# Twenty small filling matmuls instead of eight large ones at TensorE's start, and another order behind them

## The chip, the core and the metric

The kernel runs on one core of a Trainium2 chip. The metric is the time of one execution on the device, in microseconds. Lower is better. A core has five engines that run side by side, each taking its own instructions in order: TensorE (PE; its weight loads are listed as PEld), VectorE (DVE), ScalarE (ACT), GpSimd (POOL) and SyncE (SP), which here issues all transfers between HBM and the on-chip memory.

## What is computed

```python
def _attn_ref(q, k, v, f_logit):          # each [4, 8, 768, 48]
    f = 1.0 / (1.0 + np.exp(-f_logit))
    for t in range(S):
        state = f[:, :, t, :, None] * state + np.einsum('bhd,bhe->bhde', k[:, :, t], v[:, :, t])
        y[:, :, t] = np.einsum('bhd,bhde->bhe', q[:, :, t], state)
    return y

def _moe_ref(x, w_in, w_out):             # x [3072, 384], w_in [384, 2048], w_out [2048, 384]
    h = x @ w_in
    g = np.maximum(0.01 * h, h)
    return (g @ w_out).astype(np.float32)
```

A gated linear recurrence runs over 768 time steps for 4 batches and 8 heads. Its output, with the heads side by side, is the input x of a two-layer network with a leaky ReLU. Inputs and outputs are float32.

## The kernel before, in words

**Units.** The recurrence is done in chunks of 128 steps: within a chunk as a masked product of scores, between chunks by a state per head. The work is cut into 12 units j of 256 rows of x. Units 0 to 3 ("paired") hold the first two chunks of one batch each; units 4 to 11 hold one chunk of two batches.

**Steps of a unit.** Each has a short name, and the number of the unit comes next in it. `Lf`, `Lk`, `Lq`, `Lv` load f, k, q, v (SP; lines 158 and 162). `ge` and `gl` make the logarithm of the gate (ACT, 236 and 248). `cs` sums it up along time on TensorE (257 to 268), `dec` turns the sums into decays (ACT, 276 to 285). `k` and `q` scale k and q by them (301, DVE or POOL); `v` casts v (307 to 316, POOL or ACT). The scaled k and q are transposed, for units 0 to 3 on TensorE (`tk`, `tq`, line 335) with a copy from PSUM behind it (`ck`, `cq`, 348 ACT or 350 DVE), for the others by a DMA (`xk`, `xq`, 355). `sc` are the scores (371, 378), `mk` their masking (DVE, 388, 392), `pt` the chunk's addition to the state (482, 487), `sf` and `sb` the new state and its cast (497 to 508). `mx` mixes masked scores and v, and the old state (409); in a paired unit the part of the second chunk that reads the first chunk's state is a step of its own, `ms`. `xt` copies the result to xT (469 ACT, 471 DVE).

**The network.** `up_j_g` multiplies two of 16 column blocks of w_in (six matmuls of 256 columns, line 516), `pr_j_g` is the leaky ReLU (ACT, 521), `dn_j_a_n` multiplies a quarter of w_out into the output of half a (four matmuls of 384 columns, 528), `ob` copies the output (ACT 572, DVE 574), `st` stores it (578). The last half is split in two (`dh`, `oh`, `sh`; 550 to 564).

**Weights.** `WI_0` to `WI_4` load pieces of w_in of 256, 256, 512, 512 and 512 columns, `WO_0` to `WO_3` quarters of w_out. The first two pieces have buffers of their own, the others pass through a ring of three: WI_2, WI_3, WI_4, then WO_0, WO_1, WO_2, WO_3 in the slots that come free. `cw_0_c` casts 256 columns of w_in and `cw_1_c` half a quarter of w_out; the last number names the engine (0 DVE, 1 ACT, 2 POOL; lines 199 and 201). From block 2 on, an `up` needs both halves of its piece: up_j_2 and up_j_3 wait for cw_0_2 and cw_0_3.

**The filling.** `id_n@b` makes TensorE multiply a constant tile by itself, n times 128 columns into bank b, at most 512 columns in one matmul (line 207). Nothing reads the result. id_30 is thus 8 matmuls, id_1 is one.

**Order.** Nothing is scheduled by a planner at run time or by the framework: a string named `order` lists every step, and each engine gets its instructions in that order. Numbers after @ are the PSUM banks that a step writes; there are eight banks, and a step waits until the last reader of its bank is done. Every product is two TensorE instructions, a weight load and a matmul. An instruction's index below is its place in TensorE's list, counted so.

```python
    for word in order.split():
        word, _, on = word.partition("@")
        name, *numbers = word.split("_")
        parts[name](*[int(n) for n in numbers], *[int(n) for n in on.split(".") if n])
```

Of the kernel before, what the change touches and what calls it, by code (L numbers as in the profile page):

```python
# [15 lines left out]
def kernel(  # L16
# [592 lines left out]
    dec_3_0 Lf_4_1 dn_0_1_1 cw_1_5_1 cw_1_4_2 dn_1_0_1 up_0_7@1 dn_1_1_1 pr_0_7 pt_2_2@7.3 Lq_3_2 mx_2_2@6.1
    cw_1_6_1 cw_1_7_2 sf_2_0 dn_1_0_2 Lv_3_2 xt_2_0_1 k_3_1_1 dn_0_0_1 Lf_5_0 dn_1_0_3 sb_2_0_0 dn_0_1_2 Lf_5_1  # L610
    k_3_0_1 ob_1_0_1 sf_2_1 ge_4_2 tk_3_1@7 dn_0_0_2 ck_3_1_0 sb_2_1_1 Lv_4_0 ms_2 gl_4_2 dn_0_0_3 q_3_1_0
    xt_2_1_1 tk_3_0@6 q_3_0_0 ob_0_0_1 dn_0_1_3 ck_3_0_0 Lv_4_1 cs_4_0@0 ob_0_1_0 tq_3_1@3 v_3_0_0 dec_4_0
    cs_4_1@7 cq_3_1_0 tq_3_0@1 Lk_4_0 up_2_0@5 cq_3_0_0 dec_4_1 v_3_1_0 up_2_1@6 Lk_4_1 pr_2_0 dn_1_1_2 pr_2_1
    Lq_4_0 sc_3_0@4.3 ge_5_2 sc_3_1@0.1 mk_3_0_0 pt_3_2@7.5 Lk_5_0 gl_5_2 up_2_2@6 sf_3_0 dn_1_1_3 mk_3_1_1
    sb_3_0_0 Lq_4_1 pr_2_2 up_2_7@4 mk_3_1_0 ob_1_1_1 v_4_2_0 Lq_5_0 mk_3_0_1 cs_5_1@7 cs_5_0@1 pr_2_7
    dn_2_1_0@6 sf_3_1 dec_5_0 Lk_5_1 mx_3_2@0.2 k_4_2_0 sb_3_1_0 up_2_5@3 xt_3_0_0 ms_3 pr_2_5 up_2_3@4 st_0_0
    xt_3_1_0 pt_4_0@5 Lq_5_1 pt_4_1@1 pr_2_3 dn_2_0_0@0 sf_4_0 dec_5_1 q_4_2_0 dn_2_1_1 sb_4_0_0 xk_4 up_2_6@3
    sf_4_1 up_2_4@2 st_0_1 pr_2_6 sb_4_1_1 dn_2_0_1 pr_2_4 up_3_1@4 xq_4 dn_2_1_2 pr_3_1 k_5_2_0 q_5_2_1 Lf_6_0
    dn_2_0_2 Lf_6_1 dn_2_1_3 xk_5 dn_2_0_3 ob_2_1_1 up_3_0@5 ob_2_0_0 xq_5 up_3_2@7 pr_3_0 up_3_4@1 pr_3_2
    Lv_5_1 up_3_5@3 pr_3_4 ed_5 up_3_3@2 pr_3_5 sc_4_2@4.6.0.5 pr_3_3 Lv_5_0 dn_3_0_0@7 ge_6_2 mk_4_1_1  # L620
    dn_3_1_0@1 mk_4_0_1 Lf_7_0 gl_6_2 up_3_6@3 mk_4_1_0 Lf_7_1 mk_4_0_0 up_3_7@2 pr_3_6 st_1_0 dn_3_0_1 pr_3_7
    Lf_8_0 cs_6_0@5 v_5_2_0 sc_5_2@6.0.4.3 dec_6_0 Lf_8_1 cs_6_1@2 mk_5_1_0 dn_3_1_1 dec_6_1 Lk_6_1 mk_5_1_1
    dn_3_0_2 ge_7_2 mk_5_0_0 dn_3_1_2 mk_5_0_1 gl_7_2 mx_4_2@5.4 Lk_6_0 mx_5_2@3.2 Lv_6_0 xt_4_1_0 xt_4_0_0
# [30 lines left out]
    dn_10_1_1 up_11_7@2 up_10_7@6 pr_11_7 up_11_3@7 pr_10_7 up_11_0@1 pr_11_3 up_10_6@5 pr_11_0 up_11_5@3
    pr_10_6 up_11_2@2 pr_11_5 up_11_1@6 pr_11_2 up_10_4@7 pr_11_1 up_11_6@1 pr_10_4 dn_11_0_0@5 pr_11_6
    dn_10_0_2 dn_11_0_1 dn_10_1_2 dh_11_1_0@3 dn_10_1_3 oh_11_1_0_1 sh_11_1_0 dn_11_0_2 ob_10_1_0 dn_10_0_3
    st_10_1 dn_11_0_3 ob_10_0_1 dh_11_1_1 st_10_0 ob_11_0_1 st_11_0 oh_11_1_1_0 sh_11_1_1
# [35 lines left out]
```

## Time and profile before

| | |
|---|---|
| median of 3 runs | 178.19 us (177.94 to 178.99) |
| the profiled execution's own time | 178.71 us |
| its span, first to last instruction | 176.9 us |
| PE busy | 170.5 us (96%) |
| ACT busy | 122.5 us (69%) |
| DVE busy | 94.6 us (53%) |
| POOL busy | 52.5 us (30%) |
| filling matmuls (L207) | 37, 10.6 us |

Times in the profile count from the first instruction of the span. A row of the timeline has the start, the length, the engine, the line, the operation, the tiles (out<-in), the sizes and the number of instructions; what stands in brackets is the engine's idle time just before it and what ended it, where "issue" means that the engine waited for nothing that the profile shows. The chain of waits is followed back from the last instruction. Matmuls are pipelined, so their ends, and with them PE's busy time, are modelled; the start of the next matmul is the better mark.

### The profile page before, as it was taken

Reading aid. Unit: us, or ns where it says so; the run is one execution under the profiler, and the core shown is the slowest. Engines: PE = TensorE matmul, PEld = TensorE weight load, DVE = VectorE, ACT = ScalarE, POOL = GpSimd, SP = SyncE. Lnnn points to the kernel's source line nnn. Section 1 sums busy time; section 2 is a strip of 40 time slices with the busy share of each in tenths; the row PEclk is TensorE's granted clock in tenths of the full one; section 3 lists DMA queues with packets and bytes.
Section 4 is the critical chain, followed back from the end, with each engine's and each line's share of the span. In section 5 each row is a group of like instructions: output and inputs, shape, how many; then the busy total and the mean of one; then the engine's idle time right before and its main releaser. Section 6 shows DMA issues by size and latency. Waiting matters only on the chain.

```text
span 176.9 us, 5560 instructions
## 1 busy us (share of the span) xinstructions
PE 170.5 (96%) x2301; PEld 130.5 (74%) x2301; DVE 94.6 (53%) x201; ACT 122.5 (69%) x238; POOL 52.5 (30%) x102
## 2 busy tenths in 40 slices
...
GB/s 128 269 302 292 372 325 312 391 335 228 177 190 206 181 190 118 215 199 210 197 203 146 227 185 195 166 229 199 185 206 182 182 262 65 4 133 0 4 66 112
DMA packets 106856, 34.44 MB, mean 195 GB/s; under 512 B 101072, under 2 KB 105040, under 8 KB 106832
## 3 DMA queue, kind: packets, MB, share of 16 engines
...
q8 instruction: 18, 0.29, 0.7%
q14 instruction: 6, 0.05, 0.1%
...
## 4 chain that ended last, share of the span: by engine, by line
PE 89%; DMA 3%; ACT 3%; SPq 2%; issue 1%; DVE 0%; DVEq 0%
PE ps L516 36%; PE ps L528 35%; PE ps L409 6%; DMA f_raw<-in_f_logit_dram 3%; PE ps L378 3%; SPq L158 2%; PE ps L265 2%; PE ps L550 2%; PE ps L335 1%; PE ps L487 1%; PE ps L371 1%; ACT f_raw L236 1%; ACT lf L248 1%; PE ps L482 1%; PE ps L257 1%
## 5 line engine op out<-in xcount | busy, mean ns | idle before, releaser
L521 ACT ACTIVATE gT<-ps 128x512 bf16<-128x512 f32 x96 | 55.9, 602 | 24.4 <-PE ps L516 21.6
L516 PE MATMUL ps<-xT,w_in 128*128 128x256 bf16 x576 | 69.7, 273 | 0.0
L528 PE MATMUL ps<-w_out,gT 128*128 128x384 bf16 x368 | 68.4, 326 | 0.0
L516 PEld LDWEIGHTS <-w_in 128*128 128x128 bf16 x576 | 60.6, 110 | 5.3
L528 PEld LDWEIGHTS <-gT 128*128 128x128 bf16 x368 | 34.3, 98 | 18.9
L392 DVE TENSOR_TENSOR wm<-ps,ut 128x512 bf16<-128x512 f32 x32 | 20.0, 684 | 9.6 <-ACT gT L521 6.7
L307 POOL CAST vb<-v_raw 128x768 bf16<-128x768 f32 (+1 forms) x14 | 10.0, 713 | 43.5 <-DMA v_raw<-in_v_dram 43.4
L574 DVE COPY osb<-ps 128x384 f32<-128x384 f32 x12 | 6.7, 557 | 25.5 <-PE ps L528 24.8
L301 DVE TENSOR_TENSOR qh<-q_raw,at 128x384 bf16<-128x384 f32 (+1 forms) x14 | 10.3, 758 | 13.4 <-DMA q_raw<-in_q_dram 9.4
L301 POOL TENSOR_TENSOR kh<-k_raw,em 128x768 bf16<-128x768 f32 (+1 forms) x6 | 8.5, 1422 | 18.4 <-DMA k_raw<-in_k_dram 14.6
L236 ACT ACTIVATE f_raw<-f_raw 128x384 f32<-128x384 f32 (+1 forms) x16 | 10.8, 686 | 3.7 <-DMA f_raw<-in_f_logit_dram 3.7
L276 ACT ACTIVATE em<-ps 128x384 bf16<-128x384 f32 x24 | 11.8, 493 | 2.1 <-PE ps L265 0.9
L499 DVE TENSOR_TENSOR sf<-sf,ps 64x192 f32<-64x192 f32 x32 | 11.2, 350 | 3.4 <-PE ps L487 2.6
L508 POOL CAST sb<-sf 64x192 bf16<-64x192 f32 x26 | 10.3, 396 | 6.4 <-DVE sf L497 4.9
L277 ACT ACTIVATE at<-ps 128x384 bf16<-128x384 f32 x24 | 11.9, 498 | 0.0
L572 ACT COPY osb<-ps 128x384 f32<-128x384 f32 x11 | 5.3, 478 | 9.5 <-PE ps L528 8.7
L207 PE MATMUL ps<-warm 128*128 128x512 bf16 (+3 forms) x37 | 10.6, 409 | 1.1 <-DVE warm L83 1.1
L388 DVE TENSOR_TENSOR wm<-ps,pair_mask 128x512 bf16<-128x512 f32 x16 | 10.1, 685 | 2.8 <-PE ps L371 2.7
L471 DVE CAST xT<-ps 128x384 bf16<-128x384 f32 x12 | 6.5, 561 | 9.4 <-PE ps L409 9.3
L248 ACT ACTIVATE lf<-f_raw 128x384 bf16<-128x384 f32 (+1 forms) x16 | 10.8, 682 | 0.4
L505 POOL TENSOR_TENSOR sf<-sf,end 128x192 f32<-128x192 f32 x10 | 7.9, 794 | 7.1 <-PE ps L528 4.6
L469 ACT CAST xT<-ps 128x384 bf16<-128x384 f32 x12 | 6.3, 534 | 4.9 <-PE ps L409 4.9
...
## 6 DMA issues: line engine op xcount, KB each, us to landing
...
ring<-in_moe_w_out_dram SPq DMA_DIRECT2D x4, 768.0 KB, 7.3
...
ring<-in_moe_w_in_dram SPq DMA_DIRECT2D x3, 768.0 KB, 9.6
...
```

The lines of the kernel that those rows point to most:

```text
L207: nc.tensor.matmul(banks[bank][:, 0:128 * m], warm, warm[:, None, :].to_broadcast([128, m, 128]), start=True, stop=True)
L236: nc.scalar.activation(gates(j)[:, part], gates(j)[:, part], AF.Exp, scale=-1.0)
L248: nc.scalar.activation(dst, src, AF.Ln, bias=1.0)
L276: nc.scalar.activation(ems[j % 2][:, a], t[:, 0:H * D], AF.Exp, scale=1.0)
L277: nc.scalar.activation(ats[j % 2][:, a], t[:, 0:H * D], AF.Exp, scale=-1.0)
L301: eng.tensor_mul(heads(j, to[j % NR], a)[:, :, :, 0:D], raw_heads(j, x, a), decays(j, by, a))
L392: nc.vector.tensor_mul(w, src.rearrange("t (p n) -> t p n", p=P2), ut[:, None, :].to_broadcast([128, P2, 128]))
L409: nc.tensor.matmul(banks[st[j]["py", i]][32 * r:32 * r + 32, 128 * kk:128 * kk + 128], lhsT, rhs, start=(i, r) not in begun, stop=i in las ...
L499: nc.vector.tensor_add(sf[rows], sf[rows], new)
L516: nc.tensor.matmul(pm[:, i, :], w_in_of(ff, kk), xTs[j % 3][:, kk].rearrange("t a s -> t (a s)"), start=(kk == 0), stop=(kk == NK - 1))
L521: nc.scalar.activation(gTs[j % 3][:, 2 * g:2 * g + 2, :], pm, AF.Prelu, alpha=0.01)
L528: nc.tensor.matmul(po, gTs[j % 3][:, ff, 128 * a:128 * a + 128], w_out_b[quarter][:, ff % 4, :], start=(ff == 0), stop=(ff == NF - 1))
```

## The change

The first filling, one step of 30 x 128 columns in 8 matmuls, becomes 17 steps with the same columns in 20 matmuls: 16 of 128 columns, then 14 x 128 columns in four. TensorE has 12 products, 24 instructions, more before its first real one. The other fillings change too: after them all there are 45 filling matmuls instead of 37, with 13,696 columns instead of 17,024. The rest of the list has the same steps in another order, with other banks and here and there another engine: ACT gets two casts of half a v and one of a whole v more, and two xT copies and an output copy fewer; POOL gets one scaling of half a q more and one of a whole k fewer. Only the string changes. Its beginning, as far as the first two quarters of w_out, is below; the part behind it is a new order of the same steps, with no filling in either.

```diff
-    Lf_0_1 Lf_0_0 Lk_0_1 Lq_0_0 Lq_0_1 ge_0_1 Lk_0_0 gl_0_1 ge_0_0 id_30@6 cs_0_1@0 gl_0_0 dec_0_1 cs_0_0@1
-    Lv_0_2 k_0_1_0 Lf_1_2 dec_0_0 Lk_1_2 q_0_0_0 Lq_1_2 q_0_1_0 id_32@6 tq_0_0@2 k_0_0_0 cq_0_0_1 id_3@6
-    tq_0_1@3 tk_0_1@4 cq_0_1_1 tk_0_0@5 Lf_2_2 ck_0_1_0 ck_0_0_0 v_0_1_1 v_0_0_0 id_3@0 sc_0_1@6.7 sc_0_0@0.1
-    mk_0_1_1 WI_0 id_2@4 pt_0_2@2.3 mk_0_0_0 ge_1_0 sf_0_0 gl_1_0 WI_1 ge_1_1 id_13@5 cs_1_0@4 mk_0_0_1 sb_0_0_0
-    gl_1_1 mk_0_1_0 dec_1_0 id_5@7 cs_1_1@5 k_1_0_0 mx_0_2@7.0 dec_1_1 k_1_1_0 ms_0 xt_0_0_1 tk_1_0@2 Lv_1_2
-    tk_1_1@1 ck_1_0_1 q_1_0_0 xt_0_1_1 q_1_1_0 WI_2 id_7@4 tq_1_0@6 ge_2_1 cq_1_0_0 id_3@5 tq_1_1@4 WI_4 ge_2_0
-    ck_1_1_0 sf_0_1 cw_0_0_2 gl_2_0 cq_1_1_1 WI_3 sb_0_1_1 gl_2_1 id_19@2 sc_1_1@5.7 cw_0_1_1 sc_1_0@2.0
-    mk_1_1_1 cs_2_1@6 Lq_2_2 cs_2_0@1 mk_1_1_0 v_1_1_1 v_1_0_0 up_0_0@3 mk_1_0_0 dec_2_1 pt_1_2@4.7 mk_1_0_1
-    up_0_1@5 pr_0_0 Lk_2_2 sf_1_0 dec_2_0 mx_1_2@2.6 sb_1_0_1 pr_0_1 cw_0_2_0 cw_0_3_1 sf_1_1 id_16@3 ms_1
-    xt_1_0_1 sb_1_1_1 up_0_2@0 WO_0 xt_1_1_1 cw_0_7_0 up_0_3@3 pr_0_2 cw_0_6_0 up_1_1@4 pr_0_3 Lf_3_2 up_1_3@1
-    pr_1_1 cw_0_4_2 up_1_2@5 cw_0_5_1 up_1_0@7 pr_1_3 pr_1_2 up_0_6@2 WO_1 pr_1_0 up_1_6@6 q_2_0_0 pr_0_6
-    q_2_1_0 Lv_2_2 up_1_7@0 pr_1_6 k_2_1_0 up_1_5@3 pr_1_7 k_2_0_0 tq_2_0@4 pr_1_5 tq_2_1@1 cq_2_0_0 tk_2_1@5
-    WO_2 up_0_4@7 cq_2_1_0 cw_1_0_1 cw_1_1_2 ck_2_1_0 tk_2_0@2 up_1_4@6 pr_0_4 ck_2_0_0 WO_3 sc_2_1@0.3 ge_3_0
...
+    Lf_0_1 Lf_0_0 Lk_0_1 Lk_0_0 Lq_0_0 ge_0_1 Lq_0_1 gl_0_1 ge_0_0 id_1@6 id_1@6 id_1@6 id_1@6 id_1@6 id_1@6
+    id_1@6 id_1@6 id_1@6 id_1@6 id_1@6 id_1@6 id_1@6 id_1@6 id_1@6 id_1@6 id_14@6 cs_0_1@0 gl_0_0 dec_0_1
+    cs_0_0@1 Lv_0_2 k_0_1_0 Lf_1_2 dec_0_0 id_11@6 tk_0_1@2 k_0_0_0 Lk_1_2 ck_0_1_1 q_0_0_0 id_9@6 tk_0_0@3
+    Lq_1_2 ck_0_0_1 id_5@6 tq_0_0@4 q_0_1_0 cq_0_0_1 id_5@6 tq_0_1@5 Lf_2_2 sc_0_0@6.7 cq_0_1_0 v_0_0_1 v_0_1_0
+    sc_0_1@0.1 mk_0_1_1 WI_0 id_5@4 pt_0_2@2.3 mk_0_0_0 ge_1_0 mk_0_1_0 gl_1_0 Lv_1_2 ge_1_1 id_13@5 cs_1_0@4
+    sf_0_0 gl_1_1 mk_0_0_1 dec_1_0 sb_0_0_0 id_5@1 cs_1_1@5 k_1_0_0 mx_0_2@1.6 dec_1_1 k_1_1_1 xt_0_0_0 id_3@2
+    tk_1_0@0 WI_1 ms_0 q_1_1_1 xt_0_1_0 WI_2 ck_1_0_0 q_1_0_0 ge_2_0 WI_4 ge_2_1 id_21@7 tq_1_0@2 gl_2_0
+    tk_1_1@7 cw_0_0_2 cq_1_0_0 tq_1_1@4 gl_2_1 ck_1_1_0 sc_1_0@5.1 cq_1_1_1 WI_3 up_0_0@6 mk_1_0_0 v_1_1_1
+    v_1_0_0 sc_1_1@0.2 mk_1_0_1 Lk_2_2 pr_0_0 pt_1_2@7.4 cw_0_1_2 mk_1_1_1 cs_2_1@5 sf_1_0 cs_2_0@1 dec_2_1
+    mk_1_1_0 up_0_1@6 sb_1_0_0 Lq_2_2 mx_1_2@2.7 cw_0_3_1 cw_0_2_0 sf_1_1 ms_1 xt_1_0_1 up_0_2@0 pr_0_1 xt_1_1_0
+    sb_1_1_0 dec_2_0 up_0_3@5 sf_0_1 WO_0 up_1_2@2 pr_0_2 cw_0_6_2 cw_0_7_1 up_1_3@4 sb_0_1_0 pr_1_2 up_1_0@6
+    pr_0_3 up_1_7@7 pr_1_3 cw_0_5_0 up_1_1@3 pr_1_0 cw_0_4_1 up_0_6@1 pr_1_7 up_0_7@0 WO_1 pr_0_6 Lf_3_2
+    up_1_4@2 k_2_0_0 pr_1_1 k_2_1_0 Lv_2_2 up_1_6@5 pr_0_7 q_2_0_0 pr_1_4 tk_2_1@4 tk_2_0@6 q_2_1_0 ck_2_1_1
+    tq_2_0@7 up_0_5@1 ck_2_0_0 pr_1_6 cq_2_0_0 WO_2 tq_2_1@3 pr_0_5 up_0_4@0 cw_1_0_2 cq_2_1_0 cw_1_1_1
+    sc_2_0@2.4 sc_2_1@6.5 pr_0_4 mk_2_0_0 up_1_5@7 WO_3 mk_2_1_1 dn_0_1_0@1 cw_1_3_1 cw_1_2_2 mk_2_1_0
+    dn_1_1_0@3 pr_1_5 Lk_3_2 mk_2_0_1 dn_0_0_0@0 ge_3_1 ge_3_0 dn_0_1_1 gl_3_1 Lf_4_1 gl_3_0 dn_1_0_0@2 v_2_1_0
...
```

More of the change, by code (lines that the diff above doesn't have):

```diff
@@ L609 @@
[L609 to L623, printed above, removed]
@@ L654 @@
[L654 to L657, printed above, removed]
+    Lf_0_1 Lf_0_0 Lk_0_1 Lk_0_0 Lq_0_0 ge_0_1 Lq_0_1 gl_0_1 ge_0_0 id_1@6 id_1@6 id_1@6 id_1@6 id_1@6 id_1@6
@@ new lines @@
+    ge_5_2 ob_0_0_0 Lk_4_0 cs_4_1@5 pr_2_1 pt_3_2@4.3 dec_4_1 sc_3_1@1.7 Lk_4_1 sf_3_0 sc_3_0@0.6 dn_1_0_3
+    gl_5_2 mk_3_0_1 sb_3_0_0 Lq_5_0 cs_4_0@4 mk_3_1_0 ge_6_2 dn_2_1_0@5 mk_3_1_1 Lq_5_1 dec_4_0 cs_5_0@6
+    up_2_3@1 mk_3_0_0 gl_6_2 up_2_7@7 Lk_5_0 q_4_2_1 ob_1_0_0 mx_3_2@4.0 sf_3_1 pr_2_3 pr_2_7 cs_5_1@2 xt_3_0_0
+    ms_3 dec_5_0 sb_3_1_0 cs_6_1@1 Lk_5_1 xt_3_1_0 cs_6_0@3 dn_2_1_1 k_4_2_0 st_0_1 dn_2_0_0@7 dec_5_1 Lv_4_0
+    dn_2_1_2 q_5_2_0 up_2_6@4 Lv_4_1 dec_6_1 dn_2_0_1 pr_2_6 up_3_1@0 dec_6_0 up_3_0@6 xk_4 k_5_2_0 pr_3_1
@@ new lines @@
+    up_4_1@3 xt_5_1_0 Lk_6_0 sb_4_1_0 gl_7_2 sf_5_0 dn_2_0_3 Lk_6_1 pr_4_1 xt_5_0_0 up_4_4@2 sb_5_0_0 ge_8_2
+    ob_3_0_0 Lk_7_1 cs_7_1@5 sf_5_1 cs_7_0@6 pr_4_4 up_4_0@3 gl_8_2 ob_2_0_0 sb_5_1_0 up_5_1@4 pr_4_0 Lk_7_0
+    up_4_2@0 pr_5_1 q_6_2_0 cs_8_1@1 Lq_7_0 pr_4_2 dn_4_0_0@2 dec_7_0 up_5_2@7 Lq_7_1 k_6_2_1 up_4_3@3 xq_6
+    dn_4_1_0@4 pr_5_2 pr_4_3 up_5_6@0 dec_7_1 xk_6 cs_8_0@6 k_7_2_0 dn_4_0_1 dn_4_1_1 Lv_6_0 pr_5_6 Lv_6_1
+    up_5_7@7 dec_8_0 q_7_2_0 up_4_5@3 pr_5_7 st_2_0 up_5_5@5 dec_8_1 up_5_0@0 pr_4_5 xk_7 up_5_4@6 pr_5_5 pr_5_0
@@ new lines @@
+    up_4_6@7 pr_5_4 dn_4_0_2 pr_4_6 st_2_1 up_5_3@1 xq_7 sc_6_2@3.5.0.6 v_6_2_0 pr_5_3 dn_5_0_0@7 mk_6_1_1
+    Lv_7_1 dn_4_1_2 mk_6_0_0 Lv_7_0 up_4_7@1 Lf_9_1 mk_6_1_0 mk_6_0_1 dn_5_0_1 pr_4_7 ed_7 dn_5_1_0@6 pt_6_1@3
+    dn_4_1_3 Lf_9_0 sf_6_1 dn_5_1_1 ob_4_1_1 sb_6_1_1 st_3_1 dn_4_0_3 v_7_2_0 Lv_8_0 dn_5_1_2 ob_4_0_0 st_3_0
+    sc_7_2@0.5.1.3 Lk_8_0 mx_6_2@4.2 mk_7_1_1 Lv_8_1 mk_7_0_0 dn_5_1_3 xt_6_0_1 mk_7_0_1 Lk_8_1 xt_6_1_1
+    dn_5_0_2 Lq_8_0 ge_9_2 mk_7_1_0 pt_7_0@3 pt_7_1@0 pt_6_0@4 sf_7_0 ob_5_1_1 up_6_2@2 Lq_8_1 gl_9_2 sf_7_1
@@ new lines @@
+    sb_7_0_0 up_6_1@5 pr_6_2 sf_6_0 up_6_6@1 pr_6_1 sb_6_0_1 up_6_0@6 Lq_9_1 pr_6_6 v_8_2_0 cs_9_0@3 Lq_9_0
+    cs_9_1@0 pr_6_0 dn_5_0_3 dec_9_0 mx_7_2@2.4 k_8_2_1 Lk_9_0 ob_5_0_0 dn_6_1_0@5 xt_7_1_0 Lk_9_1 dec_9_1
+    xt_7_0_0 up_6_3@1 sb_7_1_0 q_8_2_0 xk_8 up_7_3@6 pr_6_3 up_6_5@7 pr_7_3 q_9_2_1 up_7_6@3 pr_6_5 up_7_0@4
+    xq_8 pr_7_6 pt_8_1@2 pt_8_0@0 pr_7_0 dn_6_0_0@1 sf_8_1 sf_8_0 dn_6_1_1 xq_9 k_9_2_1 sb_8_1_1 up_6_4@6
+    dn_6_0_1 pr_6_4 st_4_1 st_4_0 sb_8_0_0 up_7_4@7 xk_9 dn_6_0_2 pr_7_4 dn_6_1_2 Lf_10_0 up_7_1@3 Lf_10_1
@@ new lines @@
+    Lk_11_1 sf_9_1 gl_11_2 dn_7_1_3 sb_9_0_0 xt_9_0_0 Lk_11_0 xt_9_1_1 up_8_3@4 ob_7_1_1 k_10_2_0 up_8_7@0
+    sb_9_1_0 Lq_11_1 pr_8_3 cs_11_1@6 cs_11_0@5 pr_8_7 up_8_5@7 dec_11_1 up_9_3@2 Lq_11_0 pr_8_5 up_9_4@3
+    q_10_2_0 pr_9_3 xk_10 up_9_0@1 dec_11_0 up_9_7@4 pr_9_4 xq_10 k_11_2_0 pr_9_0 up_8_1@0 pr_9_7 up_9_1@6
+    pr_8_1 Lv_11_1 up_8_0@7 pr_9_1 Lv_11_0 q_11_2_0 up_8_2@2 pr_8_0 up_9_5@5 st_6_1 pr_8_2 dn_9_1_0@3 pr_9_5
+    xk_11 dn_8_1_0@1 dn_9_0_0@4 st_7_1 dn_8_1_1 up_8_6@0 up_9_2@6 xq_11 pr_8_6 v_11_2_0 up_8_4@7 pr_9_2 st_6_0
@@ new lines @@
+    up_9_6@2 pr_8_4 dn_9_1_1 pr_9_6 sc_10_2@5.0.6.7 dn_8_1_2 mk_10_0_1 dn_9_1_2 mk_10_0_0 dn_8_1_3 mk_10_1_1
+    mk_10_1_0 dn_9_1_3 ob_8_1_1 dn_9_0_1 st_8_1 ob_9_1_1 st_7_0 dn_8_0_0@2 st_9_1 dn_9_0_2 mx_10_2@0.5
+    sc_11_2@7.6.1.3 xt_10_1_1 xt_10_0_0 dn_8_0_1 mk_11_0_0 dn_9_0_3 mk_11_1_0 dn_8_0_2 mk_11_1_1 ob_9_0_1
+    mk_11_0_1 up_10_5@0 st_9_0 dn_8_0_3 pr_10_5 up_10_3@5 ob_8_0_1 mx_11_2@7.1 st_8_0 pr_10_3 up_10_1@3
+    xt_11_0_1 xt_11_1_0 up_10_7@4 pr_10_1 up_10_4@6 pr_10_7 up_11_6@0 pr_10_4 up_10_0@2 pr_11_6 up_11_1@5
```

51 lines of the change are left out of this document (19 added, 32 removed).

## The prediction

> **What bounds the kernel now.** I read the page first, then the busy time by stage, then the chain of waits at the border between the stages.
>
> ```profile
> span 176.9 us, 5560 instructions
> PE 170.5 (96%) x2301; PEld 130.5 (74%) x2301; DVE 94.6 (53%) x201; ACT 122.5 (69%) x238; POOL 52.5 (30%) x102
> q8 instruction: 18, 0.29, 0.7%
> ...
> 12.50:24.20 11.70, 9.97 (x265) 7.00 (x265) 10.22 (x25) 10.87 (x28) 1.69 (x4) 1.00 1.02 337
> 24.20:60.00 35.80, 35.80 (x527) 28.23 (x528) 22.27 (x49) 30.38 (x59) 16.41 (x31) 1.00 0.99 257
> 60.00:120.00 60.00, 60.00 (x749) 47.38 (x747) 34.43 (x60) 43.55 (x80) 21.57 (x33) 1.00 0.95 190
> 120.00:173.75 53.75, 53.72 (x652) 41.80 (x650) 17.66 (x30) 28.81 (x53) 8.65 (x13) 1.00 0.58 125
> ```
>
> The columns of the stage rows are length, then busy time of PE, PEld, DVE, ACT, POOL, granted clock, DMA share, GB/s. From 24.2 us to 173.75 us TensorE has no idle time: 149.52 of 149.55 us. Before that it waits (9.97 of 11.70 us busy in the stretch before), and a part of the busy time is the filling matmuls of L207. So the time is a sum of two: the moment T at which the dense stretch begins, and 149.6 us of work, then a tail of 3.2 us (output copy, store, end).
>
> In the border between the stages the chain of waits shows the place at which the change aims:
>
> ```profile
> 21.03 0.63 PE ps L409 x52
> 21.66 0.98 issue
> 22.64 0.30 PE ps L409 x10
> 22.95 0.97 PE ps L207 x4
> ...
> 24.20 6.67 PE ps L516 x60
> ```
>
> Inside the second mix (mx_1_2, L409) TensorE stands still for 0.98 us with "issue" as the reason: no semaphore holds it. Queue q8 brings 18 packets, 0.29 MB, that is 16 KB each; 4602 TensorE instructions over 18 packets are 256 a packet, so q8 brings TensorE's code in blocks of 256. Counting in the order, a weight load and a matmul for each product, the stall is at instruction 703: 594 come before mx_1_2, and 109 of it had been issued. Behind it comes a filling (id_16, 0.97 us) and only then ms_1 and up_0_2, the first instruction of the dense stretch, at 24.13 by the timeline.
>
> **The change, part by part.**
>
> *The sum after T.* All that TensorE does before up_0_2 is the same set of real steps in both orders, and so is all after it: 252 steps, no filling in either, and 41 changes between shapes of matmul in either order (counted). Such a change costs about 0.1 us:
>
> ```profile
> 97.29 0.65 PE ps L528 x4
> ...
> 98.49 0.89 PE ps L409 x56
> 99.38 0.76 PE ps L528 x4
> ```
>
> The same four matmuls of L528 take 0.65 us behind L516, whose tile has the same shape, and 0.76 behind a mix (L409). With equal counts the dense sum stays 149.6 us. Bounds: below, nothing, since 149.52 of it is busy; above, new waits (rivals).
>
> *The first filling.* 8 matmuls of 3,840 columns become 16 of 128 and 4 of 1,792 columns together: again 3,840 columns, 12 matmuls more.
>
> ```profile
> 1.06 3.38 PE L207 MATMUL ps<-warm 128*128 128x512 bf16 x8 [1.06 <-DVE warm L83]
> 1.46 0.15 PEld L207 LDWEIGHTS <-warm 128*128 128x128 bf16 x1 [0.28 <-issue]
> 3.99 0.52 ACT L248 ACTIVATE lf<-f_raw 128x384 bf16<-128x384 f32 x1
> 4.56 0.32 PE L257 MATMUL ps<-lf,bu 128*128 128x192 bf16 x1
> ```
>
> It ends at 4.44, the logarithm that the first cumulative sum needs at 4.51. If the extra weight loads hide, the new filling lasts 3.4 us too: cost 0. If they don't, 12 x 0.15 = 1.8 us come on top, the first sum starts 1.7 us late. I take 0: 8 x 512 columns' loads were hidden here, and eight 128-column transposes with eight loads took 0.63 us later (below), 80 ns a pair.
>
> [...]
>
> *The code block.* The 24 instructions more at the front shift all later numbers; with the other fillings changed, mx_1_2 now begins at 618 instead of 594. Instruction 703 is then the 43rd matmul of the same mix, not another step. The block edge before it, at 703 - 256 = 447, moves from the score of unit 1 (sc_1_1) to the transpose before it (tq_1_0). Before, TensorE reached that edge at 17.56 and went on at 22.64, 5.1 us later:
>
> ```profile
> 17.56 0.64 PE L371 MATMUL ps<-qT,kT 48*64 48x128 bf16 x32 [0.75 <-ACT qT L348]
> 22.35 0.69 DVE L201 CAST w_in<-ring 128x768 bf16<-128x768 f32 x1 [0.56 <-DMA ring<-in_moe_w_in_dram]
> 22.35 0.83 ACT L199 CAST w_in<-ring 128x768 bf16<-128x768 f32 x1
> 23.85 0.35 PE L409 MATMUL ps<-qT,sb 128*32 128x128 bf16 x12
> 24.13 0.30 PE L516 MATMUL ps<-xT,w_in 128*128 128x256 bf16 x1
> ```
>
> The new order reaches tq_1_0 at 16.5 (shown below), so the code is there between 21.7 (the same 5.1) and 22.64 (if the request goes out no earlier than before, or the DMA queue alone sets the time). Take the late end: 21 matmuls of the mix are left (0.3 us), then ms_1 (0.28 us, 23.85 to 24.13): 23.2.
>
> *The weights.* up_0_2 needs the third and fourth eighth of w_in (cw_0_2 on DVE, cw_0_3 on ACT in both orders). They are cast as soon as they land, at 22.35 + 0.83 = 23.18. In the load queue the same transfers stand ahead of them (only v_raw of unit 1 and WI_1 change places), so T cannot be under 23.2.
>
> *The chain of unit 1.* With these rows I follow the new order by hand:
>
> ```profile
> 8.54 0.63 PE L335 MATMUL ps<-ident,kh 128*128 128x128 bf16 x8
> 9.91 1.29 DVE L388 TENSOR_TENSOR wm<-ps,pair_mask 128x512 bf16<-128x512 f32 x2 [0.19 <-PE ps L371]
> 11.11 0.73 DVE L497 TENSOR_TENSOR sf<-ps,end 64x192 f32<-64x192 f32 x2
> 11.88 1.29 DVE L388 TENSOR_TENSOR wm<-ps,pair_mask 128x512 bf16<-128x512 f32 x2
> 13.90 0.35 PE L409 MATMUL ps<-qT,sb 128*32 128x128 bf16 x12
> 14.16 1.02 DVE L301 TENSOR_TENSOR qh<-q_raw,at 128x384 bf16<-128x384 f32 x2
> 15.44 0.42 DVE L350 COPY qT<-ps 128x512 bf16<-128x512 bf16 x1 [0.26 <-PE ps L335]
> L471 DVE CAST xT<-ps 128x384 bf16<-128x384 f32 x12 | 6.5, 561 | 9.4 <-PE ps L409 9.3
> 18.09 2.48 DVE L388 TENSOR_TENSOR wm<-ps,pair_mask 128x512 bf16<-128x512 f32 x4 [0.31 <-PE ps L371]
> ```
>
> Unit 0 comes out even: its four masks and the state add are the same 3.3 us on DVE, to 13.2, only in another order. Mix and state mix end near 14.8. Both copies of xT are now on DVE: 15.0 + 0.56 = 15.55; then the copy of k (0.42) and the scaling of q (0.51): 16.5. Hence tq_1_0 at 16.5 where it stood at 15.02 before, and the filling id_21 (1.3 us, from 14.85; its 2,688 columns at the 0.97 for 2,048 of id_16) lies under this wait. Transpose and latency 0.4, copy 0.42: score sc_1_0 at 17.4 (half of the 0.64 above), up_0_0 (0.67, sixty matmuls in 6.67) under the other half's copies, sc_1_1 at 18.5 to 18.9. Two masks (0.62 each) run meanwhile, from 17.9; the third 19.1 to 19.75, the state add 0.73, the fourth mask to 21.1. The mix takes 0.8 (52 matmuls in 0.63, 64 in all), the state mix 0.28: up_0_2 could start at 22.2. The path that ends last is therefore not this one but the weights, 23.2, or the code, 23.2. I take T = 23.25: 0.9 us before 24.13. The former filling id_16, which nothing needed once the mix was done, is what goes.
>
> Sum: the profiled execution took 178.71 (span 176.9 and 1.8 around it), 0.5 over the median 178.19. 24.13 - 23.25 = 0.9 off: 177.8 on that execution, **177.3** on the median.
>
> *Loads and stores after T.* WO_1 is moved ahead of f and v of units 3 and 2 in SP's queue and waits there for its ring slot (casts cw_0_4 and cw_0_5). That matters for a rival only. Store order and the last halves (dh_11_1_1, store) are as before, so the tail costs 0.
>
> **The rivals.**
>
> *A: the load queue, slower.* SP takes its queue in order.
>
> ```profile
> 27.54 3.97 ACT L521 ACTIVATE gT<-ps 128x512 bf16<-128x512 f32 x7
> ...
> 26.26 0.63 SPq L158 DMA_DIRECT2D f_raw<-in_f_logit_dram  x1
> 27.71 0.34 SPq L184 DMA_DIRECT2D ring<-in_moe_w_out_dram  x1
> 28.09 0.44 SPq L158 DMA_DIRECT2D v_raw<-in_v_dram  x1
> ...
> ring<-in_moe_w_out_dram SPq DMA_DIRECT2D x4, 768.0 KB, 7.3
> ...
> 30.69 0.83 POOL L201 CAST w_out<-ring 128x768 bf16<-128x768 f32 x1 [3.47 <-DMA ring<-in_moe_w_out_dram]
> 33.72 0.83 POOL L201 CAST w_out<-ring 128x768 bf16<-128x768 f32 x1 [2.20 <-DMA ring<-in_moe_w_out_dram]
> ```
>
> Before, the cast cw_0_5 on ACT released WO_1 at 27.71. In the new order cw_0_4 stands on ACT, after the cast that ends at 23.18, behind a copy of xT (0.56), six relus (0.57 each, seven in 3.97), a decay step (some 0.8) and a cast (0.83), and takes 0.83 itself; they overlap a little, so WO_1, f and v go out near 29.0, an estimate from these rows. If WO_1 then follows WO_0 (landed 30.69) as closely as a piece of its size can, it is there near 33. If it takes the full 7.3, it lands at 36.3 and its cast ends at 37.1. dn_0_1_1 needs it 13.0 us after T, at 36.2 (14 up steps 9.3, four transposes and the score 1.7, three down steps 2.0): a wait of 0.9, and as much again at the next piece, whose cast stands on ACT behind the late gates of unit 3; together 1.8, **179.1**. It decides from a landing of WO_1 after 35.4. Against it: DMA is 0.99 busy there, so transfers follow one another and do not pay their latency.
>
> *B: closer order, gain eaten.* Between two uses of a PSUM bank the order leaves work on other banks; counted in matmul steps, under 1.6 us are left at 10 places after T, 7 before, the smallest 1.1 in both. ACT carries two half casts of v and a whole one more, two xT and an output copy fewer. Some waits of 0.1 to 0.3 add up to 0.8: **178.1**.
>
> *C: the change misses its aim.* The code block still decides and comes a microsecond later: T 24.2, **178.3**. [...]
>
> *D: the filling overruns* by 1.7 us: the chain ends at 23.9 instead of 22.2, **178.0**.
>
> *E: faster.* The weights land a microsecond earlier and the code too, so unit 1's chain sets T = 22.2: **176.3**. Against it: the same bytes are ahead of them.
>
> **How the numbers follow.** Forecast (176.9 to 177.7) 0.49; B 0.16; A 0.18, of which 0.08 over 179.97, where more pieces than two come late; C 0.05; D 0.04; E 0.08. One per cent, 1.8 us, is about what a measurement tells from no change: faster 0.08 (E), slower 0.08 from A and 0.04 for a larger B, same 0.80. Range 176.7 to 179.4: it leaves out E and the dear part of A.
>
> **What would show it.** The first up_0_2 at 23.2 to 23.3 with a cast of w_in ending just before it; an "issue" gap in the second mix of 0 to 1 us after its 42nd matmul; no L207 after 16.2; PE busy without a gap from 23.3 to about 172.9. Wrong if gaps stand between 24 and 173 us, first of all before L528 at 34 to 41, or if the first sum starts after 4.7.

## The result and the profile after

The changed kernel takes 177.05 us (median of 22 runs, 176.40 to 178.74), the kernel before, beside it, 177.93 us (22 runs, 177.33 to 179.27). The ratio is 0.9949, with a 95% interval from 0.9927 to 0.9971. The profiled execution took 177.11 us. From the page of the changed kernel, the span and the largest group (busy us, mean ns, idle time ahead of it):

```profile
span 175.3 us, 5575 instructions
...
L516 PE MATMUL ps<-xT,w_in 128*128 128x256 bf16 x576 | 69.2, 273 | 0.2 <-ACT w_in L199 0.2
```

Its busy time by stage (same columns as before):

```profile
24.20:60.00 35.80, 35.80 (x527) 27.92 (x525) 22.18 (x45) 32.00 (x68) 12.74 (x24) 1.00 0.94 246
60.00:120.00 60.00, 60.00 (x794) 47.25 (x795) 34.46 (x66) 39.91 (x77) 20.81 (x33) 1.00 1.02 192
120.00:172.20 52.20, 52.10 (x608) 40.78 (x596) 15.51 (x27) 29.64 (x56) 7.25 (x12) 1.00 0.54 124
```

From 24.2 us on TensorE has no wait, as before (52.10 of 52.20 us in the last row, its work ending at 172.10). The dense stretch, from the first up_0_2 to the end of the last matmul, is 149.61 us long; it was 149.59. All the difference lies ahead of it. In TensorE's timeline:

```profile
1.06 3.38 PE L207 MATMUL ps<-warm 128*128 128x128 bf16 x20 [1.06 <-DVE warm L83]
4.46 0.32 PE L257 MATMUL ps<-lf,bu 128*128 128x192 bf16 x1
...
16.45 0.40 PE L335 MATMUL ps<-ident,qh 128*128 128x128 bf16 x4 [0.54 <-DVE qh L301]
...
21.55 0.41 PE L409 MATMUL ps<-wm,v 64*32 64x128 bf16 x16
21.89 0.35 PE L409 MATMUL ps<-qT,sb 128*32 128x128 bf16 x12
22.49 2.70 PE L516 MATMUL ps<-xT,w_in 128*128 128x256 bf16 x23 [0.25 <-ACT w_in L199]
```

and in the chain of waits:

```profile
13.19 8.39 DMA ring<-in_moe_w_in_dram
...
21.60 0.84 ACT w_in L199
...
22.49 2.59 PE ps L516 x22
```

T, the start of up_0_2, is 22.49 instead of 24.13. The second mix runs into the state mix at 21.89 without the gap of 0.98 us, no filling follows it, and up_0_2 waits 0.25 us for the cast of its weights, which starts as soon as their piece lands. In both profiled executions the time is T plus 154.6 us (178.71 - 24.13 = 154.58; 177.11 - 22.49 = 154.62). If that holds for the other runs too, the T that belongs to the median is 23.33 before and 22.45 after, an estimate from these numbers: the profiled execution of before was one of its longer ones, and the change is worth 0.88 us (177.93 - 177.05), not the 1.64 between the two profiles' T.

### The profile page after: what moved, and what is told of

Its sections match the earlier page's. It is cut to its first block, busy times and chain, and to the rows that moved or that the text cites. A ratio compares the mean times of both kernels' runs of the same rounds, so it can differ in the third digit from the quotient of the medians.

```text
span 175.3 us, 5575 instructions
## 1 busy us (share of the span) xinstructions
PE 169.3 (97%) x2309; PEld 131.3 (75%) x2309; DVE 91.7 (52%) x194; ACT 119.7 (68%) x244; POOL 51.2 (29%) x103
## 4 chain that ended last, share of the span: by engine, by line
PE 85%; SPq 7%; DMA 5%; ACT 0%; issue 0%; DVE 0%; DVEq 0%
PE ps L516 35%; PE ps L528 35%; SPq L158 6%; PE ps L409 5%; DMA ring<-in_moe_w_in_dram 5%; PE ps L378 3%; PE ps L265 2%; PE ps L550 2%; PE ps L487 1%; SPq L176 1%; PE ps L335 1%; PE ps L371 1%; PE ps L482 1%; ACT w_in L199 0%; PE ps L268 0%
## 5 line engine op out<-in xcount | busy, mean ns | idle before, releaser
L528 PE MATMUL ps<-w_out,gT 128*128 128x384 bf16 x368 | 67.3, 326 | 0.0
L521 ACT ACTIVATE gT<-ps 128x512 bf16<-128x512 f32 x96 | 55.0, 638 | 16.6 <-PE ps L516 15.1
L307 POOL CAST vb<-v_raw 128x768 bf16<-128x768 f32 (+1 forms) x11 | 8.1, 733 | 50.0 <-DMA v_raw<-in_v_dram 35.7
L574 DVE COPY osb<-ps 128x384 f32<-128x384 f32 x13 | 7.2, 556 | 23.6 <-PE ps L528 19.7
L508 POOL CAST sb<-sf 64x192 bf16<-64x192 f32 x32 | 13.1, 410 | 10.0 <-DVE sf L497 8.2
L301 DVE TENSOR_TENSOR kh<-k_raw,em 128x384 bf16<-128x384 f32 (+1 forms) x11 | 8.2, 756 | 8.8 <-ACT em L276 3.8
L471 DVE CAST xT<-ps 128x384 bf16<-128x384 f32 x14 | 7.9, 574 | 7.1 <-PE ps L409 6.7
L207 PE MATMUL ps<-warm 128*128 128x128 bf16 (+3 forms) x45 | 9.1, 347 | 1.1 <-DVE warm L83 1.1
L469 ACT CAST xT<-ps 128x384 bf16<-128x384 f32 x10 | 4.8, 499 | 7.1 <-PE ps L409 7.0
```

The source lines that it names most:

```text
L301: eng.tensor_mul(heads(j, to[j % NR], a)[:, :, :, 0:D], raw_heads(j, x, a), decays(j, by, a))
L508: eng.tensor_copy(out=sb[rows, :, y * D:y * D + D], in_=sf[rows])
L521: nc.scalar.activation(gTs[j % 3][:, 2 * g:2 * g + 2, :], pm, AF.Prelu, alpha=0.01)
L528: nc.tensor.matmul(po, gTs[j % 3][:, ff, 128 * a:128 * a + 128], w_out_b[quarter][:, ff % 4, :], start=(ff == 0), stop=(ff == NF - 1))
```

## The experiments

Ratios are to the kernel before, run on the same chip at the same time (35, 28 or 23 runs of it); 12 runs of each kernel unless said.

**The first filling alone, the order alone.** In the old order, 20 small matmuls for the 8 large ones:

```diff
-    ... ge_0_0 id_30@6 cs_0_1@0 ...
+    ... ge_0_0 (id_1@6, 16 times) id_14@6 cs_0_1@0 ...
```

> The kernel before with only the first filling changed to 20 small matmuls; id_16 stays. All later TensorE instructions move by 24: the second mix begins at index 618, index 703 is its 43rd product, and the block edge 447 lies in the filling before tq_1_1, which TensorE reached at 15.2 us in the profile before, not in the score that had to wait until 17.56. Theory M with the code asked for when TensorE comes to the edge (Ma): the code is there by 20.5, no idle time with reason issue in the second mix, mix done near 21.7, id_16, ms_1 near 23.0, T = 23.1 to 23.2: 0.9 us less than T before. Theory M with the code asked for earlier, only the queue deciding (Mb): a stall of about 1 us at the 43rd product instead of the 55th, T near 24.1, no change. Rival O: no change and no statement on the stall. If the first filling's extra loads cost time, the first cumulative sum (L257) starts after 4.7 us.

178.01 us, ratio 1.0002 [0.9978, 1.0026]: nothing. The chain of its profiled run:

```profile
21.62 0.74 PE ps L409 x61
22.36 0.97 PE ps L207 x4
23.33 0.28 PE ps L409 x12
```

The mix has no gap here, and the filling id_16 and the state mix take TensorE to 23.6.

The reverse, the new order with the 8 large matmuls:

```diff
-    ... ge_0_0 (id_1@6, 16 times) id_14@6 cs_0_1@0 ...
+    ... ge_0_0 id_30@6 cs_0_1@0 ...
```

> The changed kernel with the first filling as before, 8 matmuls; the rest of the order is the new one. The block edge 447 falls into sc_1_0 (17.36 in the profile after) instead of tq_1_0 (16.45), index 703 is again the 55th product of the second mix. Ma: the code is there 3.6 to 5.1 us after 17.36, at 21.0 to 22.4, against a need at 21.7: a stall of 0 to 0.7, of which the wait for the weights covers 0.4: time 0 to 0.4 us over the changed kernel. Rival I: the stall is back in full, 1.0, and with it 0.6 or more of time. Rival O: the time of the changed kernel.

178.32 us, ratio 1.002 [0.9996, 1.0043]. So neither half brings anything, and the two together bring 0.5%. In the chain:

```profile
20.81 0.62 PE ps L409 x41
21.43 1.51 issue
22.95 0.58 PE ps L409 x22
```

The new order's mix comes no later than with the change (by the timelines it starts at 20.49 here and at 20.89 there), and then TensorE stands for 1.5 us with nothing that the profile shows to wait for; up_0_2 starts at 23.5. The intervals of this kernel and of the changed one lie apart; their ratios differ by 0.0071, 1.26 us. Its fastest run took 177.68 us, that of the kernel before 177.33, so the loss is not that of a few unlucky runs.

**Is it the filling at the start, or the numbers?** The same 12 extra products placed in a later filling, id_21 ahead of the transposes of q, with the old first filling:

```diff
-    ... ge_0_0 (id_1@6, 16 times) id_14@6 cs_0_1@0 ...
+    ... ge_0_0 id_30@6 cs_0_1@0 ...
-    ... ge_2_1 id_21@7 tq_1_0@2 ...
+    ... ge_2_1 (id_1@7, 16 times) id_5@7 tq_1_0@2 ...
```

> The changed kernel with the first filling in 8 large matmuls, as in the run that was 1.3 us slower, but the later filling id_21 (under the wait for tq_1_0) cut into 18 matmuls instead of 6 with the same columns: 12 products more there, so that every index from tq_1_0 on is again that of the changed kernel, while the first filling is that of before. Rival I and Ma (the numbers, or where the block edge lies, matter, not the filling itself): the stall of 1.7 in the second mix is gone, T = 22.2 to 22.9, the time of the changed kernel within 0.3. If small matmuls at the start matter in themselves (clock, start of the first sum): 1.3 us over the changed kernel, as before this repair.

177.18 us, ratio 0.9956 [0.9928, 0.9985]: the change's gain is back. What counts is that the instructions from tq_1_0 on have indices 24 higher, not how TensorE starts. Its profiled run was a longer one (178.46 us). Both pieces of w_in came late in it: the mix began only at 22.07, so this profile can't show by itself that the gap is gone, and the weights landed last (chain):

```profile
22.53 0.02 issue
22.55 0.70 DVE w_in L201
```

**The filling id_16.** The prediction's gain was this filling's removal. Out of the old order alone:

```diff
-    ... cw_0_3_1 sf_1_1 id_16@3 ms_1
+    ... cw_0_3_1 sf_1_1 ms_1
```

> The kernel before without the filling id_16 between the second mix and ms_1; nothing else. Theory M (the start of up_0_2, T, is the latest of weights cast, code block and the chain of unit 1; behind it come 149.6 us whatever the order): the code still stalls the second mix if it did before, but ms_1 follows at once, T = 23.2 or, where the weights land as early as in the profile after, 22.5. Time 0.7 to 1.0 us under before, as the changed kernel. Rival O (the new order behind T is what saves): no change, within 0.2 of before. Rival I (the new indices save, the code no longer being late): the stall of 0.98 stays in this kernel, and nothing is saved beyond what the filling took; a gain of 0.9 with the stall still there would speak against I as the only cause.

177.71 us, ratio 1.0015 [0.9983, 1.0048]. The expected 0.7 to 1.0 us did not come. Its chain, then its timeline:

```profile
21.38 0.22 ACT end L279
21.60 0.48 ACT gT L521
22.08 0.73 ACT w_in L199
```

```profile
21.36 0.54 DVE L508 CAST sb<-sf 64x192 bf16<-64x192 f32 x2
...
21.80 0.50 PE L409 MATMUL ps<-qT,sb 128*32 128x128 bf16 x12
...
21.93 0.69 DVE L201 CAST w_in<-ring 128x768 bf16<-128x768 f32 x1
```

TensorE is done with the state mix near 22.1 now (21.80 and some 0.28), but the cast cw_0_3 stands on ACT behind the decays dec_2_0 and the relu pr_0_1, and cw_0_2 on DVE behind the state cast sb_1_0; they end at 22.8 and 22.6. With the filling's 0.97 us TensorE would be done at 23.05. In the old order three things end within half a microsecond: taking one away shows the next.

The same filling put into the new order, ahead of ms_1 (its bank 3 still holds a part of unit 0's product for the state, so that part of the output changes):

```diff
-    ... cw_0_2_0 sf_1_1 ms_1 xt_1_0_1 ...
+    ... cw_0_2_0 sf_1_1 id_16@3 ms_1 xt_1_0_1 ...
```

> The changed kernel with the filling id_16 (2,048 columns, 0.97 us with its shape change) put back between the second mix and ms_1. Theory M: ms_1 ends at 23.0 to 23.1 instead of 22.0, and as the weights were cast at 22.44, 0.5 to 0.6 us are lost: T = 23.05 to 23.1, time 0.5 to 0.6 over the changed kernel, and nothing of it is made up later. Rival O or I: less than 0.2.

177.88 us, ratio 0.9996 [0.9976, 1.0016]: with it the new order is no faster than the old. Here, where nothing else is late, the filling costs 0.83 us (177.88 against 177.05 us); alone it lasts 0.97. Whether its removal gains anything depends on what stands beside it.

**The second and third bound.** The old order without id_16, and on ACT the cast ahead of pr_0_1 and dec_2_0:

```diff
-    ... sf_1_0 dec_2_0 mx_1_2@2.6 sb_1_0_1 pr_0_1 cw_0_2_0 cw_0_3_1 sf_1_1 id_16@3 ms_1 xt_1_0_1 sb_1_1_1 up_0_2@0 ...
+    ... sf_1_0 mx_1_2@2.6 sb_1_0_1 cw_0_2_0 cw_0_3_1 sf_1_1 ms_1 xt_1_0_1 pr_0_1 dec_2_0 sb_1_1_1 up_0_2@0 ...
```

> The kernel before, with two edits at the border and the old indices: no id_16, and on ACT the cast cw_0_3_1 and the first copy of xT of unit 1 stand ahead of pr_0_1 and dec_2_0 instead of behind them. In the run without id_16 alone the chain ended with decays, relu, cast on ACT, up_0_2 at 22.86, although ms_1 was done at 22.1. Theory P (two bounds that lie on one another, the filling on TensorE and this queue order on ACT): together they give what neither gives alone: T = 22.2 to 22.5 where no code block is late, 0.5 to 0.8 us under before. Rival I (only the indices save): no change, or the stall of 1 to 1.7 in the second mix eats the gain. Rival O (everything behind T): no change.

177.66 us, ratio 0.9986 [0.996, 1.0012]. Timeline:

```profile
20.96 0.83 ACT L199 CAST w_in<-ring 128x768 bf16<-128x768 f32 x1 [0.44 <-DMA ring<-in_moe_w_in_dram]
...
21.14 0.54 DVE L508 CAST sb<-sf 64x192 bf16<-64x192 f32 x2
...
21.71 0.69 DVE L201 CAST w_in<-ring 128x768 bf16<-128x768 f32 x1
...
22.55 0.27 PE L516 MATMUL ps<-xT,w_in 128*128 128x256 bf16 x1 [0.47 <-DVE w_in L201]
```

ACT's cast is over at 21.8; DVE's, behind sb_1_0, now sets T, though their piece was there at 20.96. A copy of xT that the edit left late on ACT then costs another 0.25 us at 24.0. So the edit also brought a cost of its own: the time is T plus 155.0 us here (177.55 - 22.55), where it is T plus 154.6 in the profiles of the kernel before and of the changed one. With the 20 small matmuls as well:

```diff
-    ... ge_0_0 id_30@6 cs_0_1@0 ...
+    ... ge_0_0 (id_1@6, 16 times) id_14@6 cs_0_1@0 ...
```

> The same two edits and the first filling in 20 small matmuls besides, the rest in the old order. Block edge 447 lies in a filling that TensorE reaches near 15.4, long before the scores. Theory P with code asked for on arrival at the edge: never a stall in the second mix; T = 22.2 to 22.5, as the changed kernel, 0.6 to 0.9 us under before. If the old indices stalled often, this is 0.3 or more faster than the kernel without the small filling; if they did not, the two are equal within 0.2. Rival O: no change.

177.54 us, ratio 0.9999 [0.9972, 1.0026]: no difference.

Now all three queues are loosened: no id_16; on ACT the cast ahead, and the copy xt_1_1 moved to DVE; the state cast sb_1_0 on POOL, as the new order has them; first filling and indices up to the mix are the old ones:

```diff
-    ... sf_1_0 dec_2_0 mx_1_2@2.6 sb_1_0_1 pr_0_1 cw_0_2_0 cw_0_3_1 sf_1_1 id_16@3 ms_1
-    xt_1_0_1 sb_1_1_1 up_0_2@0 WO_0 xt_1_1_1 cw_0_7_0 ...
+    ... sf_1_0 mx_1_2@2.6 sb_1_0_0 cw_0_2_0 cw_0_3_1 sf_1_1 ms_1
+    xt_1_0_1 xt_1_1_0 pr_0_1 dec_2_0 sb_1_1_1 up_0_2@0 WO_0 cw_0_7_0 ...
```

> The kernel before with three edits together at the border: no id_16; on ACT the cast cw_0_3 and a copy of xT moved ahead of the leaky ReLU pr_0_1 and the decays dec_2_0 (the copy on DVE now); the state cast sb_1_0 on POOL instead of DVE. The first filling is the old one, and so are the indices up to the mix. Theory: the old order has three bounds that nearly coincide at T (start of up_0_2) of 22.75 to 23.1: the filling, ACT's order, DVE's order. Taking away one (22.78 at best) or two (22.81 at best) brought nothing; taking all three should bring T down to 22.2 to 22.6 in the undisturbed runs, ratio 0.996 to 0.998, unless the code then comes late: then an issue gap of 0.3 to 1.7 us stands in the mix and the ratio is 1.000 to 1.003. Rival: the loads alone set T; then the best T stays at 22.75 to 22.8 whatever the border's order and no gap shows.

177.24 us, ratio 0.9963 [0.9945, 0.998]. Most of the fall is there: 0.37% of the change's 0.51%, and the two intervals overlap. Timeline:

```profile
20.43 0.83 ACT L199 CAST w_in<-ring 128x768 bf16<-128x768 f32 x1
20.75 0.99 POOL L508 CAST sb<-sf 64x192 bf16<-64x192 f32 x2 [1.70 <-DVE sf L497]
...
21.11 0.69 DVE L201 CAST w_in<-ring 128x768 bf16<-128x768 f32 x1
...
21.56 0.59 PE L409 MATMUL ps<-qT,sb 128*32 128x128 bf16 x12
...
22.08 4.12 PE L516 MATMUL ps<-xT,w_in 128*128 128x256 bf16 x36
```

DVE's cast follows the state add at once, and TensorE runs from the mix into up_0_2 at 22.08 without a wait or a gap, with the old indices. The fastest run of each kernel says the same: 177.33 before, 177.34 to 177.39 in the four variants above that lack one or two of these edits or only change the start, 176.70 here, 176.40 with the change. Which of POOL's cast and DVE's copy of xT does more was not tried apart. And with the small matmuls:

```diff
-    ... ge_0_0 id_30@6 cs_0_1@0 ...
+    ... ge_0_0 (id_1@6, 16 times) id_14@6 cs_0_1@0 ...
```

> The same three edits at the border and the first filling as 20 small matmuls, so that all later indices are 24 higher. Theory: no issue gap in the mix, T 22.2 to 22.5, ratio 0.9955 to 0.9975; the difference to the run with the old first filling is what the indices are worth in the loosened border, up to 0.5 us. Rival (the loads alone set T): best T at 22.75, ratio 1.000. Rival (the rest of the new order, first batch and load queue, is needed too): ratio 0.998 to 1.000 with a cast or a copy other than the three named as the last step before up_0_2.

177.48 us, ratio 0.999 [0.9972, 1.0009]. The expected 0.9955 to 0.9975 is missed; the indices bring nothing in this order, where no gap was to be removed. On the contrary, its profiled run has a small gap that the run without the small matmuls lacks, at the 43rd product, which is instruction 703 again (timeline). It costs nothing there, since the weights decide again (chain behind it):

```profile
21.33 0.30 PE L409 MATMUL ps<-wm,vb 64*32 64x128 bf16 x10
21.83 0.24 PE L409 MATMUL ps<-wm,vb 64*32 64x128 bf16 x6 [0.20 <-issue]
```

```profile
22.00 0.02 issue
22.02 0.84 ACT w_in L199
```

They land at 22.0, 1.6 us later than in the run before, behind the same transfers. Why is open.

**Could the weights simply come sooner?** In the changed kernel, WI_2, which up_0_2 needs, ahead of WI_1:

```diff
-    tk_1_0@0 WI_1 ms_0 q_1_1_1 xt_0_1_0 WI_2 ...
+    tk_1_0@0 WI_2 ms_0 q_1_1_1 xt_0_1_0 WI_1 ...
```

> The changed kernel with WI_2 ahead of WI_1 in the load queue, nothing else. Theory W (the weights set T in the changed kernel: cast 21.60 to 22.44, up_0_2 at 22.49): the third and fourth eighth land about 1 us earlier, near 20.5, WI_1 lands about 2 us later, near 19.2, and up_0_1 starts near 20.2 instead of 20.14: T = 22.1 to 22.2, when ms_1 ends, 0.3 us faster than the changed kernel where weights were the last to come. If unit 1's chain usually ends last, no change; if the late cw_0_1 holds up_0_1 and with it the mix, up to 0.5 slower.

179.39 us (6 runs), ratio 1.0101 [1.0054, 1.0148]: slower. Chain:

```profile
21.37 0.84 POOL w_in L201
...
22.26 0.83 PE ps L516 x6
23.09 1.02 PE ps L409 x73
```

WI_1 is now late; up_0_1 stands ahead of the second mix on TensorE, so both mixes wait behind it, to 24.1. My expectation had put WI_1's landing 2 us too early.

**What is the gap?** The new order with the old first filling, whose mix had the gap of 1.5 us, and four loads (WI_4, WI_3, k and q of unit 2) issued only behind WO_0:

```diff
-    ... ge_2_0 WI_4 ge_2_1 ... cq_1_1_1 WI_3 up_0_0@6 ... Lk_2_2 pr_0_0 ... Lq_2_2 mx_1_2@2.7 ... sf_0_1 WO_0 up_1_2@2 ...
+    ... ge_2_0 ge_2_1 ... cq_1_1_1 up_0_0@6 ... pr_0_0 ... mx_1_2@2.7 ... sf_0_1 WO_0 WI_4 WI_3 Lk_2_2 Lq_2_2 up_1_2@2 ...
```

> The new order with the old first filling (which had an issue gap of 1.5 to 1.7 us in the second mix) and four loads fewer in the queue at that time: WI_4, WI_3 and k and q of unit 2 are issued only behind WO_0. Theory: the code block is late because it shares the DMA engines with a full load queue; with fewer transfers in flight the gap in the mix is gone or under 0.5 us, and T falls to 22.0 to 22.6. Later up steps of blocks 4 to 7 then wait for their pieces, so the whole time is longer by 1 to 5 us; only the border is to be read. Rival: the block is fetched at a fixed distance of instructions and takes its time whatever the load; the gap stays 1.3 to 1.7 us.

183.47 us (2 runs), ratio 1.0321 [1.0288, 1.0353]. The whole time is longer because an up step then waits 5.2 us for WI_4, a little more than expected; the border is what counts (timeline):

```profile
20.96 0.29 PE L409 MATMUL ps<-wm,v 64*32 64x128 bf16 x16
21.07 0.35 PE L409 MATMUL ps<-wm,vb 64*32 64x128 bf16 x16
21.23 0.40 PE L409 MATMUL ps<-wm,v 64*32 64x128 bf16 x16
21.56 0.35 PE L409 MATMUL ps<-qT,sb 128*32 128x128 bf16 x12
21.85 3.46 PE L516 MATMUL ps<-xT,w_in 128*128 128x256 bf16 x30
```

Same indices, and no gap: up_0_2 at 21.85 instead of 23.5. That fits a code block that is late while the load queue is full; how the loads delay it is not shown, and it is one profiled run.

The traces also date the packets of q8, which the page of before lists as "q8 instruction: 18, 0.29, 0.7%". In every run the second packet comes while TensorE works between the block edges 447 and 703 (blocks of 256 are the prediction's estimate, from 4602 TensorE instructions and 18 packets). Its start and end, and the starts of the last matmul before the edge and of the first behind it (instruction 704; the weight load 703 still runs before a gap), are, in us:

| kernel | q8 packet | last matmul before | matmul 704 |
|---|---|---|---|
| before | 20.32 to 21.27 | 21.45 | 22.65 |
| new order, 8 large matmuls | 20.65 to 21.60 | 21.22 | 22.95 |
| old order, all three and 20 small matmuls | 19.45 to 20.42 | 21.42 | 21.83 |
| changed kernel without later filling (below) | 22.70 to 23.70 | 24.28 | 25.18 |
| changed kernel | 17.97 to 18.92 | 21.46 | 21.47 |
| new order, 8 large matmuls, short queue | 18.83 to 19.90 | 21.29 | 21.31 |

In the four runs with a gap TensorE goes on 1.35 to 1.48 us after the packet's end; in each of the other ten the packet ended at least 1.41 us before matmul 704 had its turn. So in these traces the gap is the wait for this packet. With the short queue the packet starts 1.8 us earlier than with the long one, at the same indices. What the table does not explain is when the packet starts: 0.3 to 4.1 us after TensorE reaches the block edge before it, over the 14 traces.

**And the other fillings?** The changed kernel with none but the first:

```diff
-    ... id_11@6 tk_0_1@2 ... id_9@6 tk_0_0@3 ... id_5@6 tq_0_0@4 ... id_5@6 tq_0_1@5 ... id_5@4 pt_0_2@2.3 ... id_13@5 cs_1_0@4 ... id_5@1 cs_1_1@5 ... id_3@2 tk_1_0@0 ... id_21@7 tq_1_0@2 ...
+    ... tk_0_1@2 ... tk_0_0@3 ... tq_0_0@4 ... tq_0_1@5 ... pt_0_2@2.3 ... cs_1_0@4 ... cs_1_1@5 ... tk_1_0@0 ... tq_1_0@2 ...
```

> The changed kernel with no filling but the first (the 25 later matmuls left out). Theory: they only pass the time under waits; the granted clock stays 1.0, T and the whole time stay within 0.3 us of the changed kernel unless the shifted indices (50 lower) bring an issue gap of up to 1.7 us. Rival: the filling keeps the clock up; without it the granted clock in the stretch 12.5 to 24 us falls under 1.0, the products of the second mix and the first up steps take longer (over 0.115 us for 256 columns), and T rises by 0.5 us or more.

179.98 us (4 runs), ratio 1.0132 [1.0092, 1.0172]. The rival was right. Busy time by stretch, the granted clock third from the end:

```profile
5.00:7.00 2.00, 1.01 (x14) 0.70 (x11) 1.44 (x9) 2.00 (x8) 0.00 (x0) 1.00 1.10 291
7.00:9.00 2.00, 1.54 (x15) 1.04 (x15) 1.30 (x4) 1.75 (x5) 0.17 (x1) 0.61 1.15 317
9.00:11.00 2.00, 1.81 (x48) 1.54 (x48) 1.08 (x3) 1.55 (x5) 0.70 (x3) 0.50 1.09 297
...
19.00:21.00 2.00, 2.00 (x27) 1.18 (x28) 1.35 (x3) 1.28 (x4) 0.33 (x1) 0.50 1.01 352
21.00:23.00 2.00, 2.00 (x52) 1.80 (x52) 1.51 (x5) 1.18 (x3) 0.39 (x2) 0.98 1.06 398
```

The clock falls to 0.50 near 7.4 us (0.61 is the mean from 7 to 9), after a stretch in which TensorE was busy for half the time, and comes back only near 21 us. Six matmuls of up_0_0 take 1.46 us where the six of up_0_1, with the clock back, take 0.81, and the mix comes at 23.42. The timeline shows a gap again:

```profile
19.57 1.46 PE L516 MATMUL ps<-xT,w_in 128*128 128x256 bf16 x6
...
22.68 0.81 PE L516 MATMUL ps<-xT,w_in 128*128 128x256 bf16 x6
23.42 0.42 PE L409 MATMUL ps<-wm,vb 64*32 64x128 bf16 x16
...
24.27 0.24 PE L409 MATMUL ps<-qT,sb 128*32 128x128 bf16 x3
25.18 0.33 PE L409 MATMUL ps<-qT,sb 128*32 128x128 bf16 x9 [0.67 <-issue]
```

It stands in the state mix, where counting puts it: 25 products fewer move the mix from index 618 to 568, and 703 is then the 68th product, the fourth of the state mix. Three had been issued.

## Why the prediction was right, and where it was not

- **The sum after T:** right. 149.61 against 149.59 us, no wait on TensorE after up_0_2; rivals A (the load queue) and B (closer order) did not come, since the rows after 24.2 us hold no wait for either.
- **The first filling at no cost:** right. Its 20 matmuls end at 4.44 as the 8 did, and the first cumulative sum starts at 4.46; rival D did not come.
- **T:** 0.9 us off was forecast, 0.88 is what the medians show. But by the estimate above T came 0.8 lower on both sides than the working has it: 23.33 to 22.45, where the working had 24.13 to 23.25. The profiled execution of before was a long one, and its late landing (22.33) and its gap were taken for the rule. That both ends were off by the same amount, so that the difference came out, is luck. In the profile after, half of rival E happened: weights and code both came earlier than the working had them, but the weights still ended last, at 22.49 and not 22.2.
- **The weights:** right in kind. The cast of w_in ending just before up_0_2 is what the chain shows. The landing was put at 22.35 and was at 21.58; over the profiles with this load order it moves between 20.3 and 22.5, so one trace does not give it to half a microsecond. Unit 1's chain came out as worked out by hand: tq_1_0 at 16.45 (16.5), and the state mix from 21.89 would allow up_0_2 at 22.2 (22.2).
- **"The former filling id_16 is what goes":** this step failed. Taken out alone it brings nothing (1.0015), since ACT's and DVE's casts in the old list end almost as late. The prediction named the casts' engines and noted that they were the same, but not what stood ahead of them in each queue. What the change does is to loosen all three; three edits of that kind in the old order give 0.9963.
- **The code block:** this step failed too. The gap was expected in the same mix, 0 to 1 us long, and T could be no earlier than 23.2 by it. In the profile after there is none: the packet had ended at 18.92, 2.5 us before its turn, so the code bound nothing. The prediction also saw the new indices as something to be survived: instruction 703 only one step away, hence no gain. In the new order they are worth 1.26 us (against the old first filling), since without them the gap is 1.5 us; in the old order they are worth nothing. Rival C, that the code still decides and comes a microsecond later, did not come.

So the number came out although two of its steps failed. The border has several ends close together, and the working named one of them as the whole cause. What stays open: how much of the 0.5% is the border (0.37% in the old order, the intervals overlap) and how much the rest of the list; why the piece of w_in lands up to 2 us apart from run to run, and what decides when the fetch of a block begins. That the 24 instructions are worth about 1.2 us in this order is shown by the times of two kernels (0.9949 and 0.9956, against 1.002); that a lighter load queue removes the gap is one profiled run. Why the packet comes 2.7 us earlier with the 24 instructions (17.97, 20.65) is not shown: TensorE reaches the block edge before it only 0.4 us earlier (16.57, 16.97).
